# Retention and a gated MLP for eight batches on one Trainium2 core: a new hand-over table for the steady part

## The chip, the cores and the metric

One core of one Trainium2 chip. The metric is the device time of one execution in microseconds (us), as the median of several runs. A profiled execution has its own time and a span, which runs from its first to its last instruction.

## The reference, cut to what matters

```
scores = scale * q @ k.T;  ret = (scores * Dmat[h]) @ v      # per batch and head, 576 x 64, Dmat decays below the diagonal
x = ret, heads side by side                                   # 8 x 576 x 512
h = relu(x @ w_in);  u, v = halves of h                       # 512 columns each
v_n = (v - mean) / sqrt(var + 1e-6)                           # per token
v_s = w_spatial @ v_n + b_spatial
out = (u * v_s) @ w_out                                       # 8 x 576 x 512
```

## The kernel before, in words

All arithmetic is float32 accuracy. The large products are made from operands split into a rounded part ("hi") and a remainder ("lo"), with three TensorE products (hi*hi, hi*lo, lo*hi) for each.

The work of one batch falls into two parts. The retention goes over four chunks of 128 tokens and a tail of 64 tokens: scores, a mask, an update of the running state with two decays, and a "burst" (two halves of the carried state, then the values), copied out to the buffer `x32`. The gated MLP of batches 2 to 7 makes each of its three large products (kind 0: the v half, kind 1: the u half, kind 2: the output) with seven smaller products instead of eight (Strassen's scheme). For that scheme the input is cut into four quarters; three of them are split as they are (steps R for x, Y for the gated tensor g) and four are differences (steps K for x, Z for g). A difference is subtracted in place, and then it is split by a ScalarE copy to "hi" and a subtraction to "lo":

```
def split_quarter(kind, n, src, eng):
    hi, lo = right(kind, n)
    ac.copy(out=hi, in_=src)
    yield
    eng.tensor_tensor(out=lo, in0=src, in1=hi.bitcast(F32), op=ALU.subtract)
    yield
def summed_quarter(kind, n, e1=ve, e2=ve):
    a, b, t = (of_sum(kind, *k) for k in sums[n])
    e1.tensor_tensor(out=t, in0=a, in1=b, op=ALU.subtract)
    yield
    yield from split_quarter(kind, n, t, e2)
```

The order of the work is written out by hand. Every piece is a chain (a generator) that yields after each instruction or group of them. The strings `ORDER` (batch 0, batch 1, the start of batch 2) and `STEADY` (once for each of the batches 2 to 7) list names. Each occurrence of a name runs its chain one step further (function `run`), and that fixes the order of instructions on every engine: PE (TensorE), DVE (VectorE), ACT (ScalarE), POOL (GpSimd) and SP (the queue that issues all DMAs). Each engine works through its queue in order. In `STEADY`, `a` is the batch whose MLP is run, `b` is a+1, whose retention is run, and `c` is a+2, whose first chunk is begun; steps of a batch that does not exist are left out, so the pass for a=6 has no `c` and that for a=7 has neither `b` nor `c`. A trailing letter gives the engine: `v` DVE, `p` POOL, `a` ACT. The names:

- `W.a.kind.m.part`: the seven products of half m. Part A is product 1, ACT copy, product 6 on top in the same PSUM bank, copy, product 7, copy. Part B is product 5, a DVE addition (which needs A's last copy), product 3, an addition. C is product 2 and an addition, E is product 4 and an addition. For kind 2 each addition of B, C and E is followed by a DMA out.
- `v.a.n`: normalisation of token block n: relu, statistics (DVE), two ACT steps, four small DVE operations, "hi" (ACT), "lo" (DVE). `v.a.4` is the tail, with four PE steps ahead.
- `X.a.t.db`: one block of w_spatial @ v_n on PE, then u * v_s on DVE. `Y`, `Z` follow from it, `R`, `K` from `x32`.
- `k`, `q`: the decay factors on k (before the update) and on q (after the scores, before the burst). `g`: scores, mask. `p`: update, first sum, decay 1, second sum, decay 0 (the two letters are the engines of the decays). `b`: the burst. `t`, `e`: the tail's start and its end. `d`, `T`: loads.

Below, W20P6 stands for product 6 of `W.a.2.0`, and K6 sub, K6 hi, K6 lo for the steps of `K.b.6`. The four PSUM banks that `W`, `X` and `v.a.4` use are given out by the string `BANKS`, one digit per chain in the order in which the chains start: 70 digits for `ORDER`, then 33 for each full pass. The first product into a bank waits until the last reader of the chain that had the bank before is done.

A helper records every instruction, so the trace has line 164 for all of them; they are told apart by their tiles: `m` is one of the four banks, `r` a bank of the retention, `places` and `slot` the split quarters, `u` the buffer of the MLP, `x` is `x32`, `o`, `tail`, `vl` and a corner of `u` hold the output.

Of the kernel before, what the change touches and what calls it, by code (L numbers as in the profile page):

```python
# [87 lines left out]
    W.1.2.0.E K.2.6.vv W.1.2.1.E K.2.5.vp W.1.2.1.B K.2.4.pv  # L88
"""
STEADY = """  # L90
    W.a.0.0.C W.a.0.1.A W.a.0.1.C T.b W.a.0.0.A k.b.1.v b.b.0 W.a.0.0.A g.b.1 b.b.0 W.a.0.1.A W.a.0.0.C b.b.0 b.b.0
    d.b.2 p.b.1.vv W.a.0.0.A d.b.2 p.b.1.vv d.b.2 W.a.0.1.A p.b.1.vv W.a.0.0.A q.b.1.v W.a.0.0.A p.b.1.vv W.a.0.1.A
    p.b.1.vv W.a.0.0.B W.a.0.0.A W.a.0.0.E W.a.0.0.B W.a.0.1.C W.a.0.0.B W.a.0.0.E v.a.0.a W.a.0.1.E t.b.v W.a.0.0.B
    v.a.0.a v.a.2.a v.a.4 W.a.0.1.B v.a.0.a g.b.1 v.a.4 v.a.2.a W.a.0.1.A b.b.0 v.a.2.a k.b.2.v v.a.0.a b.b.1 g.b.2
    b.b.1 W.a.0.1.A W.a.0.1.B p.b.2.vv v.a.0.a q.b.2.p W.a.0.1.E b.b.1 b.b.1 v.a.4 v.a.2.a v.a.1.a d.b.3 W.a.1.0.A
    d.b.3 v.a.2.a g.b.2 d.b.3 W.a.0.1.B p.b.2.vv v.a.0.a b.b.1 v.a.4 W.a.1.0.A W.a.0.1.B W.a.1.0.C v.a.4 p.b.2.vv
    v.a.1.a W.a.1.1.C v.a.1.a W.a.1.0.A p.b.2.vv v.a.2.a v.a.4 W.a.1.0.A W.a.1.0.C b.b.2 v.a.1.a g.b.3 k.b.3.p b.b.2
    v.a.4 t.b.v v.a.4 v.a.1.a b.b.2 b.b.2 d.c.0 v.a.3.a v.a.1.a p.b.3.vp W.a.1.0.A d.c.0 v.a.3.a W.a.1.1.A W.a.1.0.A
    W.a.1.0.B W.a.1.1.A v.a.4 W.a.1.1.C W.a.1.1.A v.a.4 v.a.3.a W.a.1.0.E W.a.1.0.B v.a.4 W.a.1.0.B W.a.1.0.E
    W.a.1.1.A v.a.3.a W.a.1.1.E b.b.2 v.a.4 W.a.1.1.A v.a.3.a p.b.2.vv W.a.1.0.B v.a.4 v.a.3.a X.a.0.0 W.a.1.1.A  # L100
# [875 lines left out]
```

## Time and profile before

| | us |
|---|---|
| median of 3 runs (lowest, highest) | 525.33 (524.94, 527.98) |
| the profiled execution | 524.76 |
| its span | 523.0 |
| PE busy in the span | 490.9 |
| DVE busy | 424.5 |
| ACT busy | 253.2 |
| POOL busy | 100.8 |

The first pass of `STEADY` (a=2) begins at 164.2 us of the span, where the first product of `STEADY` follows the last one of `ORDER`; the passes for a=3 to a=7 begin at 224.8, 285.3, 345.9, 406.4 and 466.2. A busy time counts an instruction from its start to its end. Matmuls are pipelined and their ends are modelled: six products of a W step show 0.96 us, and the next step starts 0.8 us after them.

### The profile page before, as it was taken

Reading aid. Unit: us, or ns where it says so; the run is one execution under the profiler, and the core shown is the slowest. Engines: PE = TensorE matmul, PEld = TensorE weight load, DVE = VectorE, ACT = ScalarE, POOL = GpSimd, SP = SyncE. Lnnn points to the kernel's source line nnn. Section 1 sums busy time; section 2 is a strip of 40 time slices with the busy share of each in tenths; the row PEclk is TensorE's granted clock in tenths of the full one; section 3 lists DMA queues with packets and bytes.
Section 4 is the critical chain, followed back from the end, with each engine's and each line's share of the span. In section 5 each row is a group of like instructions: output and inputs, shape, how many; then the busy total and the mean of one; then the engine's idle time right before and its main releaser. Section 6 shows DMA issues by size and latency. Waiting matters only on the chain.

```text
span 523.0 us, 16887 instructions
## 1 busy us (share of the span) xinstructions
PE 490.9 (94%) x7292; PEld 468.5 (90%) x7292; DVE 424.5 (81%) x929; ACT 253.2 (48%) x533; POOL 100.8 (19%) x83
## 2 busy tenths in 40 slices
PE   0779999999999999999999999999999999999996
PEld 0668999799999999899998999899998999998996
DVE  4979988986799986989779786989779897787655
ACT  3348427554245662447326572347525373356422
POOL 2885604200013000212013000211012110120010
PEclk9999999999999999999999999999999999999999
DMA  8995413033523422153123341063221520020002
GB/s 285 409 329 182 134 45 129 1 103 101 163 77 129 156 69 83 40 184 104 42 81 112 117 140 55 29 177 128 63 83 54 170 84 0 3 90 2 1 1 91
DMA packets 29948, 55.52 MB, mean 106 GB/s; under 512 B 3249, under 2 KB 15793, under 8 KB 29618
## 3 DMA queue, kind: packets, MB, share of 16 engines
q1 hardware_dynamic: 29874, 54.45, 31.7%
q8 instruction: 57, 0.93, 0.7%
q14 instruction: 17, 0.14, 0.1%
HBM read 45.00 MB, written 9.44 MB: 104 GB/s over the span
## 4 chain that ended last, share of the span: by engine, by line
PE 70%; DVE 17%; DMA 7%; ACT 3%; issue 2%; SPq 1%; POOL 1%; ACTq 0%; DVEq 0%
PE m L164 60%; PE r L164 10%; DVE u L164 6%; DVE slot L164 2%; DMA qk<-in_qkv 2%; DVE kn L164 2%; DVE x L164 1%; DMA lent_slot<-in_w_in 1%; DMA raw<-in_w_in 1%; DMA lent_slot<-in_w_sp 1%; DMA kn<-in_qkv 1%; ACT o L164 1%; SPq L164 1%; DVE m L164 1%; DVE places L164 1%
## 5 line engine op out<-in xcount | busy, mean ns | idle before, releaser
L164 PE MATMUL m<-wsp,vn 128*128 128x288 f32 x768 | 113.8, 296 | 0.0
L164 PEld LDWEIGHTS m<-wsp,vn 128*128 128x128 f32 x768 | 105.7, 188 | 0.7
L164 DVE TENSOR_TENSOR u<-m,u 128x288 f32<-128x288 f32 (+1 forms) x104 | 44.5, 438 | 31.0 <-PE m L164 24.9
L164 ACT COPY u<-m 128x288 f32<-128x288 f32 (+1 forms) x78 | 29.9, 384 | 54.3 <-PE m L164 43.5
L164 PE MATMUL m<-slot,win 128*128 128x288 f32 x336 | 51.2, 299 | 1.8 <-DVE f L164 1.2
L164 PEld LDWEIGHTS m<-slot,win 128*128 128x128 f32 x336 | 46.1, 188 | 3.8 <-DVE f L164 1.7
L164 ACT CAST slot<-u 128x576 fp32r<-128x576 f32 x32 | 21.4, 674 | 55.5 <-DVE u L164 54.4
L164 POOL TENSOR_TENSOR places<-u,places 128x576 fp32r<-128x576 f32 x6 | 11.0, 1837 | 160.0 <-ACT places L164 160.0
L164 PE MATMUL m<-slot,wout 128*128 128x288 f32 x264 | 39.7, 297 | 0.0
L164 PE MATMUL m<-win,slot 128*128 128x512 f32 (+1 forms) x168 | 36.9, 356 | 0.0
L164 PEld LDWEIGHTS m<-slot,wout 128*128 128x128 f32 x264 | 36.2, 188 | 0.7 <-ACT u L164 0.2
L164 PE MATMUL m<-slot,part 128*128 128x288 f32 x168 | 26.7, 300 | 6.3 <-ACT o L164 6.3
L164 PE MATMUL r<-qk 64*64 64x64 f32 x960 | 21.6, 229 | 10.4 <-DMA qk<-in_qkv 10.4
L164 PEld LDWEIGHTS m<-slot,part 128*128 128x128 f32 x168 | 23.6, 188 | 7.7 <-ACT o L164 7.7
L164 ACT CAST places<-u 128x576 fp32r<-128x576 f32 x21 | 14.2, 674 | 33.5 <-DVE u L164 30.5
L164 PEld LDWEIGHTS m<-win,slot 128*128 128x128 f32 x168 | 26.8, 191 | 3.8
L164 PE MATMUL m<-quarter,slot 128*128 128x256 f32 x216 | 29.4, 285 | 0.5 <-ACT u L164 0.5
L164 PEld LDWEIGHTS m<-quarter,slot 128*128 128x128 f32 x216 | 27.8, 188 | 2.2 <-ACT u L164 0.7
L164 PEld LDWEIGHTS r<-qk 64*64 64x64 f32 x960 | 18.5, 143 | 10.8 <-DMA qk<-in_qkv 10.4
L164 DVE SCALAR_TENSOR_TENSOR u<-u,m 128x288 f32<-128x288 f32 x48 | 20.8, 451 | 8.8 <-PE m L164 8.3
L164 PE MATMUL m<-wtl,vt 128*128 128x288 f32 (+1 forms) x128 | 27.4, 295 | 0.0
L164 PE MATMUL m<-places,wout 128*128 128x288 f32 x168 | 26.6, 295 | 0.0
(162 smaller groups left out, 1160.8 us busy)
## 6 DMA issues: line engine op xcount, KB each, us to landing
qk<-in_qkv SPq DMA_DIRECT2D x30, 512.0 KB, 4.3
kn<-in_qkv SPq DMA_DIRECT2D x30, 256.0 KB, 4.9
vv<-in_qkv SPq DMA_DIRECT2D x30, 256.0 KB, 4.4
out<-o SPq DMA_DIRECT2D x32, 144.0 KB, 1.9
tail<-in_tails SPq DMA_DIRECT2D x8, 384.0 KB, 3.1
lent_slot<-in_w_in SPq DMA_DIRECT2D x4, 512.0 KB, 7.5
raw<-in_w_in SPq DMA_DIRECT2D x4, 512.0 KB, 6.9
raw<-in_w_out SPq DMA_DIRECT2D x4, 512.0 KB, 6.2
```

What stands on the lines that cost most here:

```text
L164: ins = op(*args, **kw)
```

## The change

The string `STEADY` and the digits of `BANKS` from the 75th on are replaced. `ORDER`, the chains, the tiles and the buffers stay. Both tables have 255 names and the same steps; what differs is their order, the engine letters and the banks. The letters that change:

| step | before | after |
|---|---|---|
| k.b.2 | v | p |
| q.b.1, q.b.3 | v | p |
| p.b.1 (decay 1, decay 0) | vv | vp |
| p.b.2 | vv | pp |
| t.b | v | p |
| v.a.0 (relu) | a | v |
| v.a.3 (relu) | a | p |
| Y.a.1 / Y.a.2 | p / v | v / p |
| K.b.5 (sub, lo) | vp | vv |
| K.b.6, K.b.4 | vv | pv |

```
 STEADY = """
-    W.a.0.0.C W.a.0.1.A W.a.0.1.C T.b W.a.0.0.A k.b.1.v b.b.0 W.a.0.0.A g.b.1 b.b.0 W.a.0.1.A W.a.0.0.C b.b.0 b.b.0
-    d.b.2 p.b.1.vv W.a.0.0.A d.b.2 p.b.1.vv d.b.2 W.a.0.1.A p.b.1.vv W.a.0.0.A q.b.1.v W.a.0.0.A p.b.1.vv W.a.0.1.A
...
-    X.a.1.3 e.b.v e.b.v X.a.1.2 Y.a.2.v R.b.1.v X.a.1.1 R.b.1.v X.a.1.3 Y.a.3.v Y.a.1.p K.b.5.vp Y.a.3.v W.a.1.1.B
-    Y.a.1.p X.a.1.0 K.b.7.vv k.c.0.v W.a.1.1.B X.a.1.1 W.a.2.1.A X.a.1.0 Z.a.5.vv W.a.2.1.C Z.a.7.vv Z.a.5.vv
-    W.a.2.0.A Z.a.6.vv Z.a.7.vv Z.a.5.vv Z.a.6.vv W.a.2.1.A Z.a.6.vv W.a.2.0.A p.c.0.vp W.a.2.0.C W.a.2.0.A Z.a.4.vv
-    W.a.2.0.C W.a.2.1.A R.b.2.p Z.a.4.vv W.a.2.1.C W.a.2.1.C W.a.2.0.B R.b.2.p W.a.2.0.C W.a.2.1.B g.c.0 Z.a.7.vv
...
-    W.a.2.0.B K.b.5.vp K.b.7.vv W.a.2.1.B W.a.2.0.B W.a.2.1.E K.b.6.vv K.b.4.vv W.a.2.0.E W.a.2.0.B W.a.2.0.E
-    p.c.0.vp W.a.2.0.B K.b.4.vv K.b.7.vv K.b.4.vv K.b.6.vv
+    W.a.0.1.C W.a.0.0.A W.a.0.0.C W.a.0.0.A W.a.0.1.A T.b W.a.0.0.A k.b.1.v W.a.0.0.C b.b.0 g.b.1 b.b.0 W.a.0.0.A
+    W.a.0.1.A b.b.0 b.b.0 W.a.0.1.C d.b.2 q.b.1.p p.b.1.vp d.b.2 W.a.0.0.A d.b.2 g.b.1 W.a.0.0.B p.b.1.vp W.a.0.0.A
...
+    v.a.2.a W.a.0.1.B W.a.0.1.A v.a.2.a v.a.4 v.a.0.v k.b.2.p W.a.0.1.E v.a.0.v v.a.2.a W.a.0.1.A v.a.2.a p.b.1.vp
+    W.a.0.1.A b.b.1 g.b.2 W.a.0.1.B b.b.1 v.a.0.v p.b.2.pp v.a.0.v b.b.1 b.b.1 W.a.0.1.B W.a.0.1.E d.b.3 v.a.1.a
+    d.b.3 p.b.2.pp W.a.1.0.A g.b.2 d.b.3 p.b.2.pp v.a.1.a v.a.4 q.b.2.p W.a.1.0.A v.a.4 W.a.0.1.B b.b.1 W.a.1.0.A
+    p.b.2.pp v.a.4 p.b.2.pp W.a.1.0.C v.a.4 W.a.1.0.A v.a.1.a W.a.1.0.A W.a.1.0.C v.a.4 v.a.1.a W.a.1.1.C v.a.2.a
+    v.a.4 W.a.1.1.A v.a.1.a k.b.3.p v.a.3.p v.a.2.a b.b.2 v.a.1.a g.b.3 b.b.2 v.a.4 v.a.4 p.b.3.vp W.a.1.0.A
+    W.a.1.1.A t.b.p t.b.p b.b.2 W.a.1.1.C b.b.2 W.a.1.0.B q.b.3.p d.c.0 d.c.0 b.b.2 v.a.4 W.a.1.1.A W.a.1.0.B v.a.4
...
+    e.b.v k.c.0.v X.a.1.3 X.a.1.2 e.b.v q.c.0.v W.a.1.1.B Y.a.1.v R.b.1.v X.a.0.3 R.b.1.v K.b.5.vv X.a.1.2 Y.a.3.v
+    X.a.1.0 K.b.7.vv X.a.0.3 Y.a.3.v Y.a.2.p Y.a.2.p X.a.1.1 X.a.1.0 X.a.1.1 Z.a.5.vv p.c.0.vp W.a.2.0.A W.a.2.0.C
+    Z.a.7.vv Z.a.5.vv W.a.2.0.A W.a.2.1.A Z.a.6.vv Z.a.5.vv W.a.2.1.C Z.a.6.vv W.a.2.1.A Z.a.6.vv W.a.2.1.A Z.a.4.vv
+    R.b.2.p Z.a.7.vv W.a.2.0.C Z.a.4.vv W.a.2.0.A W.a.2.1.C R.b.2.p W.a.2.1.A W.a.2.1.C W.a.2.1.B W.a.2.0.C g.c.0
+    Z.a.7.vv W.a.2.0.B Z.a.4.vv p.c.0.vp W.a.2.0.A W.a.2.1.A d.c.1 W.a.2.0.A p.c.0.vp R.b.3.v W.a.2.1.A W.a.2.1.E
+    W.a.2.0.A R.b.3.v W.a.2.1.B K.b.6.pv p.c.0.vp W.a.2.0.B W.a.2.0.B K.b.5.vv W.a.2.1.B W.a.2.1.B W.a.2.0.E
+    K.b.5.vv W.a.2.1.B W.a.2.0.B W.a.2.1.E K.b.6.pv K.b.4.pv W.a.2.0.E W.a.2.1.E K.b.7.vv W.a.2.0.B W.a.2.1.B
+    W.a.2.0.E W.a.2.0.B p.c.0.vp K.b.4.pv K.b.6.pv K.b.7.vv K.b.4.pv
 """
```

## Rows read from the trace of the kernel before

**Rows 1.** The page: busy time of the engines, the share of the span in brackets.
```profile
PE 490.9 (94%) x7292; PEld 468.5 (90%) x7292; DVE 424.5 (81%) x929; ACT 253.2 (48%) x533; POOL 100.8 (19%) x83
```

**Rows 2.** Stretches: us, busy PE, PEld, DVE, ACT, POOL, granted clock, DMA share, GB/s.
```profile
285.30:345.90 60.60, 59.59 (x919) 57.84 (x918) 50.76 (x115) 30.26 (x64) 8.51 (x7) 1.00 0.31 98
```

**Rows 3.** Waits of PE in the pass for a=2: total, times, longest.
```profile
PE m L164 <- ACT o L164: 1.0, 1, 1.0
PE r L164 <- DVE kn L164: 0.8, 1, 0.8
```

**Rows 4.** Timeline of PE, a=2, after the last X: start, duration, what.
```profile
211.49 0.96 PE L164 MATMUL m<-places,wout 128*128 128x288 f32 x6
...
213.08 0.95 PE L164 MATMUL m<-places,wout 128*128 128x288 f32 x6
...
214.59 1.06 PE L164 MATMUL m<-slot,wout 128*128 128x288 f32 x6
216.66 1.91 PE L164 MATMUL m<-slot,part 128*128 128x288 f32 x12 [1.01 <-ACT o L164]
```

**Rows 5.** Timeline of DVE, a=2, the same stretch.
```profile
207.54 0.75 DVE L164 TENSOR_TENSOR x<-x 128x576 f32<-128x576 f32 x1
...
209.04 1.99 DVE L164 TENSOR_TENSOR x<-x 128x576 f32<-128x576 f32 x1
...
212.03 0.82 DVE L164 SCALAR_TENSOR_TENSOR u<-u,m 128x288 f32<-128x288 f32 x2
212.96 2.34 DVE L164 TENSOR_TENSOR u<-u 128x576 f32<-128x576 f32 x3
...
216.04 0.76 DVE L164 TENSOR_TENSOR slot<-u,slot 128x576 fp32r<-128x576 f32 x1
...
223.77 0.89 DVE L164 TENSOR_TENSOR x<-x 128x576 f32<-128x576 f32 x1
```

**Rows 6.** Timeline of ACT, a=2, the same stretch.
```profile
214.54 1.47 ACT L164 CAST slot<-u 128x576 fp32r<-128x576 f32 x2
215.91 0.69 ACT L164 COPY o<-m 128x288 f32<-128x288 f32 x2
```

**Rows 7.** Timeline of POOL, a=2, the same stretch.
```profile
208.98 1.43 POOL L164 TENSOR_TENSOR places<-u,places 128x576 fp32r<-128x576 f32 x1 [24.35 <-ACT places L164]
...
222.59 1.45 POOL L164 TENSOR_TENSOR slot<-x,slot 128x576 fp32r<-128x576 f32 x1 [3.83 <-ACT slot L164]
224.00 1.13 POOL L164 TENSOR_TENSOR dec<-st,sd 128x256 f32<-128x256 f32 x1
```

**Rows 8.** Timeline of PE in the last pass (a=7), the steps after a wait.
```profile
469.65 3.17 PE L164 MATMUL m<-quarter,slot 128*128 128x256 f32 x24 [0.46 <-ACT u L164]
...
482.98 1.07 PE L164 MATMUL m<-slot,win 128*128 128x288 f32 x6 [0.49 <-ACT u L164]
...
485.45 1.86 PE L164 MATMUL m<-slot,quarter 128*128 128x288 f32 x12 [0.62 <-ACT u L164]
...
511.29 1.93 PE L164 MATMUL m<-slot,part 128*128 128x288 f32 x12 [1.12 <-ACT o L164]
```

**Rows 9.** Groups of ACT: busy us, mean ns of one, idle before.
```profile
L164 ACT ACTIVATE u<-u,mv 128x512 f32<-128x512 f32 x24 | 17.0, 710 | 0.0
```

**Rows 10.** Groups of DVE.
```profile
L164 DVE BATCH_NORM_STATS2 s<-u 128x6 f32<-128x512 f32 x24 | 16.4, 684 | 0.0
...
L164 DVE TENSOR_SCALAR f<-f 128x512 f32<-128x512 f32 x4 | 2.4, 610 | 0.0
```

**Rows 11.** Groups of POOL.
```profile
L164 POOL TENSOR_TENSOR qk<-qk,qs 128x512 f32<-128x512 f32 x5 | 6.4, 1280 | 63.9 <-PE r L164 63.9
...
L164 POOL TENSOR_SCALAR f<-f 128x512 f32<-128x512 f32 x4 | 6.3, 1590 | 0.0
...
L164 POOL TENSOR_TENSOR x<-x 128x576 f32<-128x576 f32 x2 | 3.3, 1668 | 4.2 <-DVE x L164 4.2
```

**Rows 12.** The page's DMA issues: KB each, us from issue to landing.
```profile
kn<-in_qkv SPq DMA_DIRECT2D x30, 256.0 KB, 4.9
```

More of the change, by code (lines that the diff above doesn't have):

```diff
@@ L90 @@
 STEADY = """
-    W.a.0.0.C W.a.0.1.A W.a.0.1.C T.b W.a.0.0.A k.b.1.v b.b.0 W.a.0.0.A g.b.1 b.b.0 W.a.0.1.A W.a.0.0.C b.b.0 b.b.0
-    d.b.2 p.b.1.vv W.a.0.0.A d.b.2 p.b.1.vv d.b.2 W.a.0.1.A p.b.1.vv W.a.0.0.A q.b.1.v W.a.0.0.A p.b.1.vv W.a.0.1.A
-    p.b.1.vv W.a.0.0.B W.a.0.0.A W.a.0.0.E W.a.0.0.B W.a.0.1.C W.a.0.0.B W.a.0.0.E v.a.0.a W.a.0.1.E t.b.v W.a.0.0.B
-    v.a.0.a v.a.2.a v.a.4 W.a.0.1.B v.a.0.a g.b.1 v.a.4 v.a.2.a W.a.0.1.A b.b.0 v.a.2.a k.b.2.v v.a.0.a b.b.1 g.b.2
-    b.b.1 W.a.0.1.A W.a.0.1.B p.b.2.vv v.a.0.a q.b.2.p W.a.0.1.E b.b.1 b.b.1 v.a.4 v.a.2.a v.a.1.a d.b.3 W.a.1.0.A
@@ L96 @@
[L96 to L100, printed above, removed]
@@ L101 @@
-    p.b.3.vp X.a.0.2 t.b.v p.b.3.vp X.a.0.0 W.a.1.1.B X.a.0.3 W.a.1.1.B W.a.1.1.E p.b.3.vp X.a.0.1 q.b.3.v g.b.3
-    X.a.0.3 X.a.0.2 Y.a.2.v b.b.3 g.c.0 b.b.3 b.b.3 q.c.0.v X.a.0.1 b.b.3 X.a.1.2 d.c.1 d.c.1 e.b.v d.c.0 b.b.3
-    X.a.1.3 e.b.v e.b.v X.a.1.2 Y.a.2.v R.b.1.v X.a.1.1 R.b.1.v X.a.1.3 Y.a.3.v Y.a.1.p K.b.5.vp Y.a.3.v W.a.1.1.B
-    Y.a.1.p X.a.1.0 K.b.7.vv k.c.0.v W.a.1.1.B X.a.1.1 W.a.2.1.A X.a.1.0 Z.a.5.vv W.a.2.1.C Z.a.7.vv Z.a.5.vv
-    W.a.2.0.A Z.a.6.vv Z.a.7.vv Z.a.5.vv Z.a.6.vv W.a.2.1.A Z.a.6.vv W.a.2.0.A p.c.0.vp W.a.2.0.C W.a.2.0.A Z.a.4.vv
@@ L106 @@
-    W.a.2.0.C W.a.2.1.A R.b.2.p Z.a.4.vv W.a.2.1.C W.a.2.1.C W.a.2.0.B R.b.2.p W.a.2.0.C W.a.2.1.B g.c.0 Z.a.7.vv
-    p.c.0.vp W.a.2.1.A W.a.2.0.A W.a.2.1.A d.c.1 p.c.0.vp Z.a.4.vv W.a.2.0.A R.b.3.v W.a.2.1.A W.a.2.1.E p.c.0.vp
-    R.b.3.v W.a.2.1.B W.a.2.1.B W.a.2.1.B K.b.5.vp W.a.2.0.A K.b.6.vv W.a.2.1.E W.a.2.0.B W.a.2.0.E W.a.2.1.B
-    W.a.2.0.B K.b.5.vp K.b.7.vv W.a.2.1.B W.a.2.0.B W.a.2.1.E K.b.6.vv K.b.4.vv W.a.2.0.E W.a.2.0.B W.a.2.0.E
-    p.c.0.vp W.a.2.0.B K.b.4.vv K.b.7.vv K.b.4.vv K.b.6.vv
+    W.a.0.1.C W.a.0.0.A W.a.0.0.C W.a.0.0.A W.a.0.1.A T.b W.a.0.0.A k.b.1.v W.a.0.0.C b.b.0 g.b.1 b.b.0 W.a.0.0.A
@@ new lines @@
+    W.a.0.1.A b.b.0 b.b.0 W.a.0.1.C d.b.2 q.b.1.p p.b.1.vp d.b.2 W.a.0.0.A d.b.2 g.b.1 W.a.0.0.B p.b.1.vp W.a.0.0.A
+    p.b.1.vp W.a.0.0.E b.b.0 W.a.0.0.B v.a.4 p.b.1.vp W.a.0.0.E W.a.0.0.B v.a.0.v W.a.0.1.A W.a.0.0.B v.a.0.v
+    v.a.2.a W.a.0.1.B W.a.0.1.A v.a.2.a v.a.4 v.a.0.v k.b.2.p W.a.0.1.E v.a.0.v v.a.2.a W.a.0.1.A v.a.2.a p.b.1.vp
+    W.a.0.1.A b.b.1 g.b.2 W.a.0.1.B b.b.1 v.a.0.v p.b.2.pp v.a.0.v b.b.1 b.b.1 W.a.0.1.B W.a.0.1.E d.b.3 v.a.1.a
+    d.b.3 p.b.2.pp W.a.1.0.A g.b.2 d.b.3 p.b.2.pp v.a.1.a v.a.4 q.b.2.p W.a.1.0.A v.a.4 W.a.0.1.B b.b.1 W.a.1.0.A
@@ new lines @@
+    p.b.2.pp v.a.4 p.b.2.pp W.a.1.0.C v.a.4 W.a.1.0.A v.a.1.a W.a.1.0.A W.a.1.0.C v.a.4 v.a.1.a W.a.1.1.C v.a.2.a
+    v.a.4 W.a.1.1.A v.a.1.a k.b.3.p v.a.3.p v.a.2.a b.b.2 v.a.1.a g.b.3 b.b.2 v.a.4 v.a.4 p.b.3.vp W.a.1.0.A
+    W.a.1.1.A t.b.p t.b.p b.b.2 W.a.1.1.C b.b.2 W.a.1.0.B q.b.3.p d.c.0 d.c.0 b.b.2 v.a.4 W.a.1.1.A W.a.1.0.B v.a.4
+    v.a.3.p W.a.1.0.E W.a.1.1.A v.a.4 v.a.3.p W.a.1.0.B W.a.1.0.E W.a.1.1.A v.a.3.p W.a.1.1.B W.a.1.0.B v.a.3.p
+    W.a.1.1.E v.a.3.p X.a.0.0 W.a.1.1.A W.a.1.1.B p.b.3.vp W.a.1.1.E X.a.0.2 p.b.3.vp g.b.3 t.b.p p.b.3.vp X.a.0.0
@@ new lines @@
+    X.a.0.1 X.a.0.1 X.a.0.2 b.b.3 g.c.0 b.b.3 b.b.3 b.b.3 X.a.1.3 d.c.1 d.c.1 d.c.0 e.b.v b.b.3 Y.a.1.v W.a.1.1.B
+    e.b.v k.c.0.v X.a.1.3 X.a.1.2 e.b.v q.c.0.v W.a.1.1.B Y.a.1.v R.b.1.v X.a.0.3 R.b.1.v K.b.5.vv X.a.1.2 Y.a.3.v
+    X.a.1.0 K.b.7.vv X.a.0.3 Y.a.3.v Y.a.2.p Y.a.2.p X.a.1.1 X.a.1.0 X.a.1.1 Z.a.5.vv p.c.0.vp W.a.2.0.A W.a.2.0.C
+    Z.a.7.vv Z.a.5.vv W.a.2.0.A W.a.2.1.A Z.a.6.vv Z.a.5.vv W.a.2.1.C Z.a.6.vv W.a.2.1.A Z.a.6.vv W.a.2.1.A Z.a.4.vv
+    R.b.2.p Z.a.7.vv W.a.2.0.C Z.a.4.vv W.a.2.0.A W.a.2.1.C R.b.2.p W.a.2.1.A W.a.2.1.C W.a.2.1.B W.a.2.0.C g.c.0
@@ L111 @@
+    Z.a.7.vv W.a.2.0.B Z.a.4.vv p.c.0.vp W.a.2.0.A W.a.2.1.A d.c.1 W.a.2.0.A p.c.0.vp R.b.3.v W.a.2.1.A W.a.2.1.E
+    W.a.2.0.A R.b.3.v W.a.2.1.B K.b.6.pv p.c.0.vp W.a.2.0.B W.a.2.0.B K.b.5.vv W.a.2.1.B W.a.2.1.B W.a.2.0.E
+    K.b.5.vv W.a.2.1.B W.a.2.0.B W.a.2.1.E K.b.6.pv K.b.4.pv W.a.2.0.E W.a.2.1.E K.b.7.vv W.a.2.0.B W.a.2.1.B
+    W.a.2.0.E W.a.2.0.B p.c.0.vp K.b.4.pv K.b.6.pv K.b.7.vv K.b.4.pv
 """
-BANKS = "0123102302013322103101030130131301232121333303031310302301321032101023203121312032302201302012013200312132010201321231130231301302133201021303130210120023120230231022130310232023103013312013123120311023203121312032302201302012013200312132010201321231130231301302133201"
+BANKS = "0123102302013322103101030130131301232121333303031310302301321032101023203132023132312021321231023103012312023132023203130230320132012103203132023132312021321231023103012312023132023203130230320132012103203132023132312021321231023103012312023132023203130230320132012103"
```

## The prediction, made before the changed kernel was run

> **What bounds the kernel now.** I read the page first, then the busy time by stretch, the waits of PE, and the timelines of one full pass and of the last one. The page has PE busy for 94% of the span, DVE for 81% [rows 1]. In the full pass for a=4 PE is busy 59.6 of 60.6 us at clock 1.00, while DVE has 9.8 us and POOL 52 us idle [rows 2]. So the steady part is bound by PE's own work, which both tables share: the same products, and in both eleven changes between retention and MLP products. Only PE's waits can be won, and only new ones lost. One full pass has one wait of size: 1.0 us on an ACT copy of `o`; a=2 has a further 0.8 us on `kn` [rows 3]. It is the second product of part A of kind 2 (product 6). PE could have issued it at 214.59 + 0.80 = 215.39 and did at 216.66 [rows 4], so it costs 1.27 us (more than the idle shown, since ends are modelled). Product 6 needs Z6 hi and lo and the copies of product 1. DVE does three subtractions Z5, Z7, Z6 from 212.96 to 215.30 and Z6 lo from 216.04 to 216.80 [rows 5]; ACT has the Z casts up to 216.01 and only then the two copies, to 216.60 [rows 6]. DVE came to Z5 late because K7 sub took 1.99 us instead of 0.75 [rows 5] while POOL ran Y1 lo [rows 7]. The last pass, with no retention beside it, has four waits of 0.46 to 1.12 us [rows 8].
>
> **The change, part by part.**
>
> *The Z wait in the passes a=2 to 5.* In the new table the last X (X11) is followed on PE by the update of c.0, W20P1, W20P2, W21P1, W21P2 and then W21P6. Counting from the end of X11: the update with its change of tile shape costs 0.71 (213.08 + 0.80 to 214.59), four steps at 0.795 cost 3.18 [rows 4], so W21P6 may be issued at 3.89, and its second matmul, the first to need Z6 lo, at 4.02. DVE takes X11 from 0.06 to 0.51 (0.45 each in rows 5), Z5 starts 0.11 later as it did before, at 0.62, the three subtractions end at 2.96 and Z6 lo 1.50 after that (215.30 to 216.80 before), at 4.46 [rows 5]. The copy of W21P1 stands behind Z6 hi on ACT, as before [rows 6], and ends near 4.0. So the loss is about 4.5 - 4.02 = 0.48 instead of 1.27, a gain of 0.8 a pass. What shortens it: only one X stands between PE and Z5, and Y2 lo, now on POOL, runs beside DVE steps that read PSUM. Four passes: -3.2 us. Bounds: a loss from 0 to the old 1.27, so -5.1 to 0; I take the worked-out value.
>
> *a=6 and Z in a=7.* There is no c, so the update is missing: loss 0.48 + 0.71 = 1.19 against 1.27 to 1.28 before (511.29 in rows 8). I count nothing.
>
> *The `kn` wait of a=2 [rows 3].* The update of b.1 stands one product (0.71) later in the new table, while k.b.1 still follows T.b and the last K steps on DVE. -0.7 us; bounds -0.8 and 0.
>
> *The last pass (a=7).* It is the table with the retention left out, so products it separated become neighbours. Before, the three waits on `u` cost 0.46, 0.49 and 0.62 [rows 8] and 0.16 each of modelled end: 2.05 us. In the new order I find three. W00P6 is followed directly by W00P7, as such a pair was before: 0.6. W01P3 follows W01P7 directly and needs its copy and then a DVE addition: 0.16 + 0.37 + 0.42 and three hand-overs of some 0.05, 1.1. W10P5 takes the bank of W10's part A, whose last copy stands on ACT behind the tail's normalisation. From the start of W01P3 on, with 0.71 for a large ACT step [rows 9], 0.68 and a small sum for statistics [rows 10], 0.35 to 0.40 for a copy [rows 6] and 0.2 to 0.3 for a small step, that runs vn lo 0 and the addition (DVE, to 1.4), relu u1 (ACT, 2.1), its statistics (3.0), the copy of W10P6 (3.95), its two ACT steps (4.9), the tail's relu (5.5), statistics (6.5), two ACT steps (7.5) and the copy, 7.85; PE is there after 6.4. That is 1.4; in a full pass 2.2 us of retention lie between and cover it. Together 3.1, so +1.05 us; bounds -1 (half of them covered) and +2.5.
>
> *Engines.* On DVE the pass loses k.b.2, q.b.1, q.b.3 and two subtractions (0.75 for 576 columns [rows 5], so 0.67 for the 512 of a k or q), three decays and the tail's factor of 256 columns (0.4 each, from 0.45 for 288 in rows 5), and gains K5 lo (0.75) and a relu (610 ns [rows 10]): some -3.9 us. ACT loses two relus. POOL goes from 6 to 15 operations, from 8.5 us [rows 2] to about 19, at 1.28 for a q, 1.67 for an `x`, 1.59 for the relu [rows 11]. None of this is on PE's path by itself, and I cost it at nothing; the covers are these. k.b.2: the load is issued 0.4 after the burst of b.0, lands in 4.9 [rows 12], POOL takes 1.3, and the update comes 1.5 us after that. The relu of v.a.3: about 1.9 us before its statistics would be due, and 0.9 more before X00 reaches vn lo 3. K6 sub and K4 sub, from DVE to POOL: K6 lo ends near 2.4 us after the last W20P3 and W00P6 needs it at 3.0. The tight bank: W21P4 waits for the copy of W21P7 with one product between, 0.68 of 0.80.
>
> *POOL beside DVE.* One POOL operation held a DVE operation with two SBUF inputs for 1.24 us [rows 5, 7]. Between two POOL operations in a row the waiting DVE operation went first: it started at 223.77, took 0.89 [rows 5], and the POOL operation recorded from 224.00 took 1.13 [rows 7]. So a held DVE operation waits for the rest of one POOL operation, not for the queue, and in the dense stretch from Z5 to k.b.1 I count two holds, 0.95 us together, which the covers above contain. The Trainium skill, "SBUF — State Buffer", section "SBUF: two separate sides", says that the pair of ports that the two engines share is locked for a whole instruction and the loser blocks fully; the trace agrees (1.99 against 0.75 us). It speaks against a table that gives POOL more, and it stands behind the third rival.
>
> *The sum*, against the profiled execution: 524.76 - 3.2 - 0.7 + 1.05 = 521.9 us. The median shown lies 0.57 above that execution, so 522.5.
>
> **The rivals.** *The gain is taken back.* A place with little cover (W21P4 with 0.1, W10P5 with some 0.9, K6 lo with 0.6) comes late in each pass and costs the 0.8 that Z gives: 522.5 + 3.2 = 525.7, within 0.1% of before. For it: the covers are thin, and I worked them out by hand. Against: DVE and ACT have less to do.
>
> *No wait left.* If the Z chain runs 0.5 us quicker and the last pass loses no more than before: 522.5 - 4 * 0.48 - 1.05 = 519.5. For it: PE's floor is that low. Against: three dependent subtractions, a cast and a lo stand in a row whatever else is done, and their pace was the same in each pass.
>
> *Slower: POOL holds DVE.* In the stretch from Z5 to k.b.1 DVE has no idle time, and the new table has four POOL operations there (R2 lo, K6 sub, K4 sub, decay 0). If three or four of them hold a DVE operation for the full 1.24, that is 3.7 to 5.0 instead of the 0.95 counted. k.b.1 ends some 1.45 before the update needs it, so 1.3 to 2.6 us a pass reach PE, five times: 529 to 535.5. It decides from 1.45 us of further holds a pass. For it: [rows 5, 7] show a full hold. Against: most DVE steps beside them read PSUM, and the same stretch before had three POOL operations, two of them in rows 7, with no wait of PE behind it.
>
> That the order is not what is written is excluded, since the helper fixes the program order.
>
> **How the numbers follow.** The forecast (Z wait halved, a dearer last pass) gets 0.57, with its own range 520.0 to 524.5 from the bounds of its terms. Gain taken back 0.18, no wait left 0.12, POOL holds 0.13. One per cent is 5.25 us, about what a measurement of this kernel can tell from no change. Faster than 520.1 is most of the second rival and the edge of the forecast: 0.12. Slower than 530.6 is the greater part of the third: 0.10. The rest, 0.78, is within 1%. The range 519.0 to 529.0 leaves out the dearer holds and a little below.
>
> **What would show it.** Right: in each full pass a wait of PE at W21P6 of some 0.3 to 0.5 us, no `kn` wait in a=2, pass length near 59.8 us instead of 60.5, POOL busy near 19 us a pass, DVE near 47, and in a=7 waits at W01P3 and W10P5 of about 1 us. Wrong: a pass longer than 60.5 us, PE waiting on `kn`, on K6 lo or on a bank in every pass, or `x` and `slot` operations of DVE that take 2 us beside POOL.

## The result, and the profile after

The changed kernel takes 519.82 us (median of 4 runs, 519.34 to 520.60) beside 525.13 us (median of 4) for the kernel before: ratio 0.989, 95% interval 0.985 to 0.993. That is 5.3 us or 1.1% faster, where 2.6 us were forecast. The time lies inside the range, 0.8 us above its lower end. The profiled execution took 519.81 us with a span of 517.7 us (524.76 and 523.0 before).

The page's busy times answer to [rows 1], and the busy time by stretch of the pass for a=4 (same columns) to [rows 2].

```profile
PE 488.4 (94%) x7292; PEld 465.3 (90%) x7292; DVE 407.6 (79%) x895; ACT 243.5 (47%) x521; POOL 147.9 (29%) x129
```

```profile
283.10:342.50 59.40, 59.30 (x919) 57.48 (x918) 46.85 (x108) 28.70 (x63) 17.46 (x15) 1.00 0.31 100
```

Both stretches are as long as a pass. PE has the same 919 matmuls in the second, which is 1.2 us shorter (1.12 by the table below). DVE gave up 3.9 us and POOL took 9.0 us more. PE is still the engine without idle time.

The pass lengths come from the timeline of PE: a pass begins with its first block of 24 kind-0 matmuls. By this mark the first pass of the kernel before begins at 163.29, not at the 164.2 given ahead of the prediction.

| us | starts at | a=2 | a=3 | a=4 | a=5 | a=6 | a=7 to the end |
|---|---|---|---|---|---|---|---|
| before | 163.29 | 61.49 | 60.55 | 60.51 | 60.54 | 59.82 | 56.76 |
| after | 162.84 | 59.76 | 59.42 | 59.39 | 59.42 | 59.58 | 57.29 |
| difference | -0.45 | -1.73 | -1.13 | -1.12 | -1.12 | -0.24 | +0.53 |

The differences add up to 5.26 us, which is the difference of the two spans. The first column is the part of the program that both kernels share. In the profiles of this case it ends anywhere from 162.79 to 165.35, so its 0.45 us is not the change's.

Now the place that the forecast was about. The timeline of PE in the pass for a=2, after the last X, answers to [rows 4].

```profile
210.17 0.69 PE L164 MATMUL r<-vv,kn 64*64 64x64 f32 x32
210.79 1.06 PE L164 MATMUL m<-places,wout 128*128 128x288 f32 x6
211.69 0.96 PE L164 MATMUL m<-slot,wout 128*128 128x288 f32 x6
212.48 0.95 PE L164 MATMUL m<-places,wout 128*128 128x288 f32 x6
213.27 0.95 PE L164 MATMUL m<-slot,wout 128*128 128x288 f32 x6
214.16 2.22 PE L164 MATMUL m<-slot,part 128*128 128x288 f32 x12
216.23 1.75 PE L164 MATMUL m<-places,part 128*128 128x288 f32 x12
```

PE comes to product 6 at 214.16 instead of 216.66 and begins with a delay of only 0.1 us. But its block of 12 shows 2.22 us where the next one shows 1.75. No idle time stands beside it: the wait is inside the block, after its first matmul. The chain of waits over the same stretch (start, duration, what) names what ended it.

```profile
210.27 0.47 DVE u L164
...
210.76 0.77 DVE u L164
...
211.55 0.77 DVE u L164
...
212.35 0.77 DVE u L164
...
213.14 0.68 ACT slot L164
...
213.84 0.77 DVE slot L164
...
214.66 3.45 PE m L164 x24
```

Read downwards this is X11, the subtractions Z5, Z7, Z6, then Z6 hi on ACT and Z6 lo on DVE. Z6 lo ends at 214.61, and the second matmul of product 6 starts 0.05 us later. From start to start the first and second matmul lie 0.49 us apart instead of 0.13. Before, the last matmul of W20P2 and the first of product 6 lay 1.30 us apart. The same 0.49 us stands in each of the passes for a=2 to 7. DVE no longer comes late to Z5: in the timeline of DVE every subtraction of that stretch is at its own length again, against the 1.99 us in [rows 5].

```profile
205.92 0.75 DVE L164 TENSOR_TENSOR x<-x 128x576 f32<-128x576 f32 x1
...
210.76 2.34 DVE L164 TENSOR_TENSOR u<-u 128x576 f32<-128x576 f32 x3
...
213.84 0.76 DVE L164 TENSOR_TENSOR slot<-u,slot 128x576 fp32r<-128x576 f32 x1
```

Last, the timeline of PE in the last pass, the steps after a wait, beside [rows 8].

```profile
464.62 1.68 PE L164 MATMUL m<-quarter,slot 128*128 128x256 f32 x12 [0.52 <-ACT u L164]
...
472.37 0.97 PE L164 MATMUL m<-quarter,places 128*128 128x256 f32 x6 [0.92 <-DVE u L164]
...
480.02 1.86 PE L164 MATMUL m<-slot,quarter 128*128 128x288 f32 x12 [0.99 <-ACT u L164]
...
505.46 2.23 PE L164 MATMUL m<-slot,part 128*128 128x288 f32 x12 [0.76 <-ACT o L164]
```

The first three are W00P7, W01P3 and W10P5, the three places that the forecast named. The fourth is product 6 of kind 2, where the update of a next batch is missing.

### The profile page after: what moved, and what is told of

Same layout as the page of the kernel before. It is cut to its first block, busy times and chain, and to the rows that moved or that the text cites. A ratio compares the mean times of both kernels' runs of the same rounds, so it can differ in the third digit from the quotient of the medians.

```text
span 517.7 us, 16872 instructions
## 1 busy us (share of the span) xinstructions
PE 488.4 (94%) x7292; PEld 465.3 (90%) x7292; DVE 407.6 (79%) x895; ACT 243.5 (47%) x521; POOL 147.9 (29%) x129
## 4 chain that ended last, share of the span: by engine, by line
PE 74%; DVE 14%; DMA 5%; ACT 3%; issue 1%; POOL 1%; SPq 1%; ACTq 0%; POOLq 0%; DVEq 0%
PE m L164 64%; PE r L164 10%; DVE u L164 5%; DVE slot L164 2%; DMA lent_wout<-in_qkv 1%; DMA lent_slot<-in_w_in 1%; DMA raw<-in_w_in 1%; ACT slot L164 1%; DMA lent_slot<-in_w_sp 1%; SPq L164 1%; DVE m L164 1%; DVE places L164 1%; ACT vn L164 1%; POOL wsp L164 1%; DVE kn L164 1%
## 5 line engine op out<-in xcount | busy, mean ns | idle before, releaser
L164 POOL TENSOR_TENSOR slot<-u,slot 128x576 fp32r<-128x576 f32 x8 | 11.6, 1448 | 145.7 <-ACT slot L164 126.3
L164 ACT COPY u<-m 128x288 f32<-128x288 f32 (+1 forms) x78 | 28.6, 380 | 36.2 <-PE m L164 30.7
L164 ACT COPY r<-warm 1x2 f32<-1x2 f32 x32 | 4.9, 152 | 58.2 <-PE r L164 58.0
L164 PE MATMUL m<-slot,part 128*128 128x288 f32 x168 | 28.0, 302 | 2.1 <-ACT o L164 1.5
```

Source lines behind the costliest of these rows:

```text
L164: ins = op(*args, **kw)
```

## The experiments

The theory after the result: the order of the steps around the last X sets the time, by how much work PE has between that X and product 6, and the engine letters only keep POOL from holding DVE (a hold is a DVE step that becomes longer because it waits for a POOL step). The rivals: the letters themselves, through DVE's 17 us less of work, or the last pass. The times of before beside the runs were 526.21 us (27 runs), 526.05 (11) and 526.12 (23) in the three groups, so that runs are compared by ratios to before. The digits of `BANKS` go with the order in every run, so the runs cannot tell the two apart. Where pass lengths are given below, they go from one Z5 on DVE to the next, which is what the expectations use; by that mark before has 60.5 and the changed kernel 59.4 us in the passes from a=2 on.

### The old order with the new engines

```
-    d.b.2 p.b.1.vv W.a.0.0.A d.b.2 p.b.1.vv d.b.2 W.a.0.1.A p.b.1.vv W.a.0.0.A q.b.1.v W.a.0.0.A p.b.1.vv W.a.0.1.A
+    d.b.2 p.b.1.vp W.a.0.0.A d.b.2 p.b.1.vp d.b.2 W.a.0.1.A p.b.1.vp W.a.0.0.A q.b.1.p W.a.0.0.A p.b.1.vp W.a.0.1.A
...
-    Y.a.1.p X.a.1.0 K.b.7.vv k.c.0.v W.a.1.1.B X.a.1.1 W.a.2.1.A X.a.1.0 Z.a.5.vv W.a.2.1.C Z.a.7.vv Z.a.5.vv
+    Y.a.1.v X.a.1.0 K.b.7.vv k.c.0.v W.a.1.1.B X.a.1.1 W.a.2.1.A X.a.1.0 Z.a.5.vv W.a.2.1.C Z.a.7.vv Z.a.5.vv
```

> The old table with the thirteen engine letters of the new one; order and banks as before. Order theory (the gain comes from what stands between the last X and W21P6 and from the later update in a=2): the only help here is that Y1 lo leaves POOL and no longer holds K7 sub, 1.24 us less on DVE against 0.68 more for Y1 lo, so the Z wait falls by about 0.55 us a pass and the kn wait of a=2 stays: 522.0 to 523.0 us. Engine theory (the gain comes from DVE having 3.9 us less to do in a pass): nearly the whole gain, 520 to 521 us.

Measured: 526.76 us, ratio 1.0008 (0.9987 to 1.0028), slower than both cases of the expectation. There is no gain, so the letters alone are not it. The passes from a=2 on did shorten, to 59.9 to 60.3 us, with the wait before product 6 at 0.66 us from start to start instead of 1.30. That was lost again in one place, the first retention of the pass for a=2. The rows are from the timelines of DVE, POOL and PE, and below them the busy time by stretch:

```profile
165.26 2.64 DVE L164 TENSOR_TENSOR slot<-x,slot 128x576 fp32r<-128x576 f32 x2
167.82 1.75 DVE L164 TENSOR_TENSOR kn<-kn,kd 128x512 f32<-128x512 f32 x1
...
167.25 1.77 POOL L164 TENSOR_TENSOR qk<-qk,qs 128x512 f32<-128x512 f32 x1
...
169.62 0.69 PE L164 MATMUL r<-vv,kn 64*64 64x64 f32 x32 [1.83 <-DVE kn L164]
170.25 4.62 PE L164 MATMUL m<-quarter,slot 128*128 128x256 f32 x24
```

```profile
170.30:172.00 1.70, 1.70 (x12) 1.70 (x10) 1.27 (x3) 0.33 (x1) 0.19 (x1) 0.58 0.95 343
172.00:174.00 2.00, 2.00 (x12) 2.00 (x11) 0.00 (x0) 0.42 (x2) 1.89 (x3) 0.50 0.41 151
```

The decay factor on q, now on POOL, begins at 167.25, while the last of DVE's subtractions is still running. The factor on kn on DVE begins at 167.82 beside it and takes 1.75 us, 0.68 without such a neighbour, and PE waits 1.83 us. Right behind that wait the granted clock is 0.58 and then 0.50, the lower of PE's two levels, 1.2 GHz, until about 174, and 24 matmuls take 4.62 us.

### The same, but the factor on q of chunk 1 stays on DVE

```
-    d.b.2 p.b.1.vp W.a.0.0.A d.b.2 p.b.1.vp d.b.2 W.a.0.1.A p.b.1.vp W.a.0.0.A q.b.1.p W.a.0.0.A p.b.1.vp W.a.0.1.A
+    d.b.2 p.b.1.vp W.a.0.0.A d.b.2 p.b.1.vp d.b.2 W.a.0.1.A p.b.1.vp W.a.0.0.A q.b.1.v W.a.0.0.A p.b.1.vp W.a.0.1.A
```

> The old order with the new engine letters, but the decay factor on q of chunk 1 stays on DVE as in the kernel before. If the loss of the old order with all new letters came from that one POOL operation, which held the factor on kn: the wait of PE on kn in a=2 is 0.8 us again instead of 1.8, the granted clock stays 1.00 after it, the pass of a=2 is 62.0 to 63.0 us from Z5 to Z5 instead of 64.8, and the time is 523.3 to 524.5. If it is not that operation but the other moved ones (k.b.2, the decays, K6 and K4 sub): wait and clock as with all letters new, time 526 to 527.

Measured: 523.92 us, ratio 0.9964 (0.9945 to 0.9984), as the first case had it. The timeline of PE at the same place:

```profile
168.29 0.69 PE L164 MATMUL r<-vv,kn 64*64 64x64 f32 x32 [0.77 <-DVE kn L164]
168.92 3.11 PE L164 MATMUL m<-quarter,slot 128*128 128x256 f32 x24
```

The wait is 0.77 us again, the granted clock of the two stretches is 1.00, the 24 matmuls take 3.11 us, and a=2 is 62.62 us from Z5 to Z5 (64.84 with the letter). One POOL step in a bad place had cost the whole gain of all other letters. In the changed kernel the same letter does no harm: there the factor on kn starts at 167.45 and q on POOL at 167.55, so that q is the second of the two (kn takes 0.68 us and q 1.71), and the update stands a product later.

### The new order with the old engines

```
-    W.a.0.1.A b.b.0 b.b.0 W.a.0.1.C d.b.2 q.b.1.p p.b.1.vp
+    W.a.0.1.A b.b.0 b.b.0 W.a.0.1.C d.b.2 q.b.1.v p.b.1.vv
...
-    W.a.2.1.B K.b.6.pv p.c.0.vp W.a.2.0.B W.a.2.0.B K.b.5.vv
+    W.a.2.1.B K.b.6.vv p.c.0.vp W.a.2.0.B W.a.2.0.B K.b.5.vp
```

> The new table and banks with the thirteen engine letters of the old one. Order theory: Z5 still starts right after the one last X, so the wait at W21P6 stays near 0.5 us and there is no kn wait in a=2: 519.5 to 521.0 us. Engine theory: without the relief of DVE the time goes back to 524 to 525.5 us.

Measured: 522.71 us, ratio 0.9926 (0.9898 to 0.9953), between the two cases. The order with its banks alone brings 0.7 of the 1.0%. What is missing are single waits, not the same in every pass. The one in a=2, from the timelines of DVE, POOL and PE:

```profile
178.79 1.50 DVE L164 TENSOR_TENSOR dec<-st,sd 128x256 f32<-128x256 f32 x1
...
178.73 1.27 POOL L164 TENSOR_TENSOR qk<-qk,qs 128x512 f32<-128x512 f32 x1 [9.72 <-PE r L164]
...
180.68 0.97 PE L164 MATMUL m<-quarter,places 128*128 128x256 f32 x6 [0.89 <-DVE u L164]
```

A decay of 0.41 us takes 1.50, since POOL began its factor on q 0.06 us before, and an addition behind it on DVE comes 0.9 us late for PE. The passes are 59.5 us, but that for a=5 is 60.40: there `dec` takes 1.31 us beside a POOL factor on kn, and PE waits 0.60. With the new letters these decays stand on POOL, in one row with q and kn, and run there at 0.61 us each, so that neither meets the other.

### The old kernel with the engines of Y1 and Y2 exchanged

```
-    X.a.0.3 X.a.0.2 Y.a.2.v b.b.3 g.c.0 b.b.3 b.b.3 q.c.0.v X.a.0.1 b.b.3 X.a.1.2 d.c.1 d.c.1 e.b.v d.c.0 b.b.3
-    X.a.1.3 e.b.v e.b.v X.a.1.2 Y.a.2.v R.b.1.v X.a.1.1 R.b.1.v X.a.1.3 Y.a.3.v Y.a.1.p K.b.5.vp Y.a.3.v W.a.1.1.B
+    X.a.0.3 X.a.0.2 Y.a.2.p b.b.3 g.c.0 b.b.3 b.b.3 q.c.0.v X.a.0.1 b.b.3 X.a.1.2 d.c.1 d.c.1 e.b.v d.c.0 b.b.3
+    X.a.1.3 e.b.v e.b.v X.a.1.2 Y.a.2.p R.b.1.v X.a.1.1 R.b.1.v X.a.1.3 Y.a.3.v Y.a.1.v K.b.5.vp Y.a.3.v W.a.1.1.B
```

> The old table with only Y1 lo moved from POOL to DVE and Y2 lo from DVE to POOL. Order theory: K7 sub takes 0.75 us instead of 1.99, DVE comes to Z5 about 0.55 us sooner and the Z wait of five full passes falls from 1.27 to some 0.7 us: 522.0 to 523.0 us. Engine theory: the same amount of work on each engine, so no change: 524.6 to 525.6 us. If the hold was no part of the wait: no change either, with K7 sub short and the wait as before.

Measured: 523.73 us, ratio 0.9946 (0.9927 to 0.9964), between the cases and nearer to the first. Timelines of DVE and PE, a=2:

```profile
209.34 0.75 DVE L164 TENSOR_TENSOR x<-x 128x576 f32<-128x576 f32 x1
...
211.95 2.34 DVE L164 TENSOR_TENSOR u<-u 128x576 f32<-128x576 f32 x3
...
215.65 1.93 PE L164 MATMUL m<-slot,part 128*128 128x288 f32 x12 [0.37 <-ACT o L164]
```

K7 sub is at 0.75 us instead of 1.99, the wait before product 6 falls from 1.30 to 0.66 us in the passes for a=2 to 5, and the passes to 59.9 us (that for a=3 has 60.57). So Y1 lo on POOL was some 0.6 us of the loss in each of these passes (1.24 us of hold gone, 0.67 for Y1 lo on DVE added), and one exchanged pair of letters is half of what the change won.

The reading of [rows 5, 7] has the cause right, but the step that it names is held in a=2 only. In the passes for a=3 to 5 of the kernel before, K7 sub and Y1 lo begin together. K7 sub keeps its 0.75 us, POOL takes 2.04 us instead of 1.43, and the step held is the next one, the factor on kn, with 1.92 us instead of 0.68. Timelines of DVE and POOL of the kernel before, a=3:

```profile
269.59 0.75 DVE L164 TENSOR_TENSOR x<-x 128x576 f32<-128x576 f32 x1
270.26 1.92 DVE L164 TENSOR_TENSOR kn<-kn,kd 128x512 f32<-128x512 f32 x1
...
269.59 2.04 POOL L164 TENSOR_TENSOR places<-u,places 128x576 fp32r<-128x576 f32 x1 [24.43 <-ACT places L164]
```

The pass for a=6 has no such factor, and there the next two DVE steps read PSUM and take 0.46 us each beside POOL. Nothing is held, and the exchange wins nothing: 59.83 us before and 59.77 after, with product 6 starting 1.42 and 1.35 us after the matmul ahead of it.

### The changed kernel with the update ahead of the last X

```
-    X.a.1.0 K.b.7.vv X.a.0.3 Y.a.3.v Y.a.2.p Y.a.2.p X.a.1.1 X.a.1.0 X.a.1.1 Z.a.5.vv p.c.0.vp W.a.2.0.A W.a.2.0.C
+    X.a.1.0 K.b.7.vv X.a.0.3 Y.a.3.v Y.a.2.p Y.a.2.p p.c.0.vp X.a.1.1 X.a.1.0 X.a.1.1 Z.a.5.vv W.a.2.0.A W.a.2.0.C
```

> The new table with the update of c.0 moved one X forward, so that it no longer stands between X11 and W21P6. Order theory: 0.71 us of PE work less covers the Z chain, so the loss at W21P6 grows from 0.48 to about 1.19 us in the passes a=2 to 5 (a=6 and a=7 have no such update): 2.8 us slower than the changed kernel, 522.3 to 523.0 us. If PE's total work alone sets the time, or DVE's load: as the changed kernel, 519.3 to 520.3 us.

Measured: 525.11 us, ratio 0.9980 (0.9961 to 0.9998), slower than either case. Timeline of PE, a=2:

```profile
210.79 0.69 PE L164 MATMUL r<-vv,kn 64*64 64x64 f32 x32
211.41 1.87 PE L164 MATMUL m<-wsp,vn 128*128 128x288 f32 x12
...
217.48 1.70 PE L164 MATMUL m<-slot,part 128*128 128x288 f32 x8 [0.76 <-ACT o L164]
```

A single step of 0.7 us of PE, moved by one place, takes back most of the change. The passes are 60.25, 60.23 and 60.25 us, 0.83 longer, and over the whole steady part that is 3.4 of the 4.8 us that the change won there. The rest of the lost time is in the profile's first part, which ends at 165.35 here and which the edit does not touch. The passes are longer because product 6 now waits twice, at its first matmul (1.05 us from start to start) and again at its second (0.49). The passes for a=6 and 7, which have no such update, stay as they were. What counts is how much PE has to do behind the last X.

### The lo parts read last

The wait that is left stands at the second matmul, the first that reads Z6 lo. Here the two matmuls of each small product that read the data's lo part come at its end; the sum is the same, in another order. Shown is the branch for kinds 1 and 2; for kind 0, where the data is the other operand, the same is done.

```
...
-            pe.matmul(ps, ws[0], rs[0], start=start and k == 0, stop=False, skip_group_check=True)
-            pe.matmul(ps, ws[0], rs[1], start=False, stop=False, skip_group_check=True)
-            pe.matmul(ps, ws[1], rs[0], start=False, stop=stop and k == 1, skip_group_check=True)
+                early += [(ws[0], rs[0]), (ws[1], rs[0])]
+                late += [(ws[0], rs[1])]
+        every = early + late
+        for i, (x, y) in enumerate(every):
+            pe.matmul(ps, x, y, start=start and i == 0, stop=stop and i == len(every) - 1, skip_group_check=True)
```

> The changed kernel with the six matmuls of each small product in another order: the two that read the lo part of the data come last. Order theory: in W21P6 it is the second matmul that waits 0.36 us for Z6 lo in every pass; as the fifth it has 0.4 us more, and only the wait of the first for the ACT copy is left (0.1 in a=2 to 5, 0.9 in a=6 and a=7): 1.5 to 2.2 us faster than the changed kernel, passes of 59.1 us. If Z6 hi or the copy ends last: no change.

Beside it ran the changed kernel itself:

> The changed kernel itself, once more, as the one to compare the next three with on the same chip. Ratio to the kernel before about 0.989; passes of 59.4 us.

Measured: 519.55 us, ratio 0.9856 (0.9828 to 0.9884), against 521.07 us and 0.9901 (0.9879 to 0.9923): 1.5 us faster, as forecast. Timeline of PE, a=2:

```profile
214.63 1.87 PE L164 MATMUL m<-slot,part 128*128 128x288 f32 x12
216.34 1.75 PE L164 MATMUL m<-places,part 128*128 128x288 f32 x12
```

The passes are 59.03 us, 0.35 shorter, and no wait of size is left in a=2 to 5. That is the floor of this order, and the wait at the second matmul was its last loss.

### The same in the kernel before

> The kernel before, old table and old engines, with only the two matmuls of each small product that read the data's lo part put last. In the old order W20P6 waits at its first matmul for the ACT copy of W20P1, which ends at 216.60, and Z6 lo ends at 216.80, some 0.2 us later than that. If the order of the steps is what decides where the wait falls: hardly any gain, passes 60.2 to 60.5 us, the wait on the ACT copy stays at 1.0 us of idle, time 524.5 to 526.0. If the lo parts alone made the passes long, in whatever order: passes 59.5 to 60.0 us and a time of 521 to 523.

Its edit is the same as the one above. Measured: 525.70 us, ratio 0.9991 (0.9971 to 1.0010). Timeline of PE, a=2:

```profile
218.15 1.87 PE L164 MATMUL m<-slot,part 128*128 128x288 f32 x12 [1.00 <-ACT o L164]
```

Nothing is won, the passes stay at 60.5 us (one has 60.85): in the old order the copy ends the wait 0.2 us before Z6 lo is there, and to ask for Z6 lo later helps nobody. The same edit is worth 0.35 us a pass behind one order and nothing behind the other.

### A table of its own for the last pass

```
-        run(STEADY, b)
+        run(LAST if b == B - 1 else STEADY, b)
```

`LAST` is the new table with the steps of the other batches left out and the steps from W00 to W11 put so that other products stand before W00P7, W01P3 and W10P5. The part of it that decides:

```
+    W.a.0.0.B v.a.0.v v.a.2.a W.a.0.1.B v.a.2.a W.a.0.1.B v.a.4 v.a.0.v W.a.0.1.E v.a.0.v v.a.2.a v.a.2.a W.a.0.1.E
+    v.a.0.v v.a.0.v W.a.0.1.B v.a.1.a W.a.1.0.A v.a.1.a v.a.4 v.a.4 W.a.1.0.A W.a.0.1.B W.a.1.0.A v.a.4 W.a.1.0.C
```

> The changed kernel with a table of its own for the last pass (a=7): W01P6 moved between W00P6 and W00P7, W01P7 moved two products forward so that W01P4 and v.a.4 stand between it and W01P3, and the ACT copy of W10P7 put ahead of vn hi 2. Order theory: the three waits of the last pass that the missing retention leaves open (together 2.9 us of PE's time) go, and little comes in their place: 2.0 to 2.9 us faster than the changed kernel. If they are only moved (the normalisation of the tail sets the end of this stage in any order): 0 to 0.7 us faster, with the wait ahead of X00.

> Both edits of c2 and c3. If they touch different waits, their gains add: 3.5 to 5 us faster than the changed kernel. If one takes over the other's wait: little more than the better of the two.

In both kernels the copy of W10P7 stands ahead of the last two steps on token block 2, so that in batch 7 a part of the normalised v (288 columns of that block) is computed from other numbers; the amount of work is the same. Measured: 520.39 us, 0.9886 (0.9859 to 0.9914), and with the lo parts last 517.90 us, 0.9842 (0.9814 to 0.9870). The last pass gains only 0.5 us in both, so by the passes the two gains add; together they are 3.2 us, less than the 3.5 to 5 expected. Timeline of PE of the first of the two, the steps after a wait:

```profile
471.41 0.97 PE L180 MATMUL m<-quarter,places 128*128 128x256 f32 x6 [0.60 <-DVE u L180]
...
474.52 1.06 PE L180 MATMUL m<-slot,quarter 128*128 128x288 f32 x6 [0.41 <-ACT u L180]
...
480.39 1.06 PE L180 MATMUL m<-slot,quarter 128*128 128x288 f32 x6 [0.85 <-ACT u L180]
```

The wait at W00P7 is gone, that at W01P3 is smaller, and that at W10P5 has moved to the product behind it (W11P6). A new one came at W10P6: there is one chain of small steps on DVE and ACT in this pass, and PE meets it somewhere.

A second try at the table, with every step reading what it reads in the steady table, and the lo parts last. One line of it, against the first try:

```
-    v.a.0.v v.a.0.v W.a.0.1.B v.a.1.a W.a.1.0.A v.a.1.a v.a.4 v.a.4 W.a.1.0.A W.a.0.1.B W.a.1.0.A v.a.4 W.a.1.0.C
+    v.a.0.v W.a.0.1.E W.a.0.1.B v.a.2.a v.a.2.a W.a.1.0.A W.a.1.0.A v.a.1.a v.a.4 v.a.4 v.a.1.a W.a.0.1.B W.a.1.0.A
```

> The changed kernel with the two matmuls of each small product that read the data's lo part put last, and with a table of its own for the last pass in which other steps stand between W00P6 and W00P7, and between W01P7 and W01P3 with its addition, and every copy and statistic reads what it reads in the steady table. If waits on ACT and DVE set the length of the last pass: three waits of about 1 us become small, Z5 of a=7 to the end of that pass's W kind 0 and 1 products shortens by some 1.0 us against the changed kernel with lo last alone, and the time is 518.0 to 518.8. If these waits only move, because the normalisation of the last pass (relu, statistics, scale, hi, lo on ACT and DVE) has no other work beside it: 519.3 to 519.8, as with lo last alone. In all other passes Z5 to Z5 is 59.0 us.

Measured: 516.58 us (516.26 to 516.90), ratio 0.9814 (0.9791 to 0.9838), below both cases of the expectation. The waits at W00P7 and W01P3 are gone. Two are left, at W10P6 and at W11P6:

```profile
472.35 1.07 PE L180 MATMUL m<-slot,quarter 128*128 128x288 f32 x6 [1.00 <-ACT u L180]
...
478.00 1.06 PE L180 MATMUL m<-slot,quarter 128*128 128x288 f32 x6 [0.63 <-ACT u L180]
```

From Z5 to Z5 the last interval is 52.24 us, against 53.14 with the lo parts last alone: a gain of 0.9 us, so about a third of the waits of the last pass could be covered. The time fell by more. Between the two profiled executions the rest is the unchanged first part, which was short here: it ends at 162.79 in this profile and at 163.41 in that of the lo parts alone. The medians lie 3.0 us apart, and what more is in them is not shown. This version beats both kernels; it is 1.9% faster than before, where the changed kernel is 1.0 to 1.1%.

## Why the prediction was right, and where it was wrong

The way of the change and its main mechanism were right, but only half of its size was forecast. The median lies just below the 520.0 to 524.5 that the forecast gave itself, in the tail below 520.1 to which the text gave a chance of 0.12.

**What bounds the kernel.** Right, but for the words that both tables share PE's own work (see the floor). PE is as busy as before. DVE's 3.9 us less a pass came out as counted, POOL has 17.5 us where 19 were counted, and neither shows in the time by itself: in the old order all letters but one give a ratio of 0.9964 (0.9945 to 0.9984), no better than the one exchanged pair with 0.9946 (0.9927 to 0.9964). The eleven changes between retention and MLP products are ten in the traces, and ten in both tables.

**The Z wait, a=2 to 5.** The best of the terms. Forecast were 3.89 us from the end of X11 to product 6, 4.46 to the end of Z6 lo, and a loss of 0.48. Measured from the start of the update, which is that end: 214.16 - 210.17 = 3.99, 214.61 - 210.17 = 4.44, and a loss of 0.46: product 6 begins 0.10 late, and its second matmul follows 0.49 us behind the first, 0.36 more than the normal 0.13. Moving the update back and exchanging only Y1 and Y2 show both causes that the text named, the filler behind the last X and the hold by Y1 lo. That the step held is K7 sub was read from one pass, and the other passes hold the factor on kn in its place.

**What the forecast missed: the floor.** The wait explains 0.81 of the 1.12 us that a pass gained. The sentence that failed is that PE's own work is the same in both tables. Taking from a pass what its wait adds to the normal spacing of matmuls leaves 60.53 - (1.30 - 0.13) = 59.36 us for the old order and 59.41 - (0.49 - 0.13) = 59.05 for the new, and the lo parts read last give 59.03 as a measured length. The new order's floor is 0.3 us lower, with the old engines too. It is made of pieces of some 0.1 us. One can be named: between two of the tail's matmuls (`m<-win,xt`) the old order has 0.34 us from start to start in each of the passes for a=2 to 6, in every run with that order, where the new one has 0.24. What causes the others, and whether it is the order or the banks, stays open. Over the five passes this is 1.4 us of what was missing.

**`kn` in a=2.** Right: the wait is gone, and this pass gained 1.73 us = 0.81 + 0.3 + some 0.6, with -0.7 forecast.

**a=6.** Right for the wait: before 1.42 us from start to start, after 1.05 at the first matmul and 0.49 at the second, 1.29 and 1.28 us above the normal spacing. The 0.24 that it gained anyway would be the floor.

**The last pass.** The mechanism was right and the size off. The three waits stand where they were put and cost 0.67 + 1.08 + 1.14 = 2.9 us above the normal spacing, 3.1 forecast. Before, there were four such places with 0.62 + 0.15 + 0.65 + 0.78 = 2.2 us and not three with 2.05, so the term is +0.7 instead of +1.05; the lower floor takes a part of that, and the pass lost 0.53. For W10P5 the forecast had a chain of small steps on DVE and ACT that ends in a copy 7.85 us after the start of W01P3. The timeline of ACT has that copy end at 479.57 + 0.39 = 479.96, which is 7.59 us after 472.37:

```profile
479.57 0.39 ACT L164 COPY u<-m 128x288 f32<-128x288 f32 x1
```

**The rest** of the difference is the first part's 0.45 us, which no step of the change reaches, and the 0.57 us by which the median was taken to lie above the profiled execution; after the change it lies on it.

**The rivals.** *Gain taken back* did not happen: W21P4, W10P5 in the full passes and K6 lo all came in time. *No wait left* has the time of the result, 519.5, but not its reason: the wait was there in every pass. It needed another order of matmuls inside a product to go. *POOL holds DVE* did not decide, though holds are there: two steps of DVE in the stretch, 1.05 and 0.98 us where 0.75 is normal, 0.5 us together where 0.95 were counted. That it is a real danger is shown by the old order with the new engines, where one hold of 1.07 us (1.75 - 0.68) cost 2.2 us of its pass (64.84 - 62.62), with the clock behind it. The Trainium skill, "SBUF — State Buffer", section "SBUF: two separate sides", says that the two engines lock their shared ports for a whole instruction; the 1.50 us of `dec` beside a POOL step of 1.27 agree.

## What to carry to other kernels

When an engine waits for a chain on other engines, count what it has to do between the chain's start and its end: one step of 0.7 us on the right side of the chain's start was here worth 3.4 of the 4.8 us that the change won in the steady part. Read more than one pass: the cause was the same in the others, but another step was held. Look for the wait inside a block as well, where the profile shows a longer block and no idle time, and feed late operands to the last matmuls of the product. And put steps of DVE and POOL that read SBUF in sequence on one of the two engines rather than side by side on both.

## What was not expected of the hardware

A wait of PE of 1.83 us, behind the small matmuls of the retention, was followed by some 3.5 us at a granted clock of 0.5 to 0.6 (the lower level, 1.2 GHz), while one of 0.77 us at the same place left it at 1.00. The 24 matmuls behind it took 4.62 - 3.11 = 1.5 us longer, beside the 1.06 us by which the wait itself had grown. One profile of each shows it.

The length of a POOL step in a profile also holds its own wait. Where a DVE step with two SBUF inputs was already running, POOL's step came out longer and DVE's did not. Y1 lo took 2.04 us instead of 1.43 when K7 sub began with it. The factor on q took 1.77 us in the old order with the new engines, where a subtraction on DVE ran until 167.90, and 1.27 us in the new order with the old engines, where only small steps ran on DVE when it began. So of two such steps the second one was held, on whichever engine it stood.
